# Rounding w_in's blocks on GpSimd, and the first residual and the second solver put earlier

## The chip, the cores and the metric

The kernel runs on one core of a Trainium2 chip. The metric is the device time of one execution in microseconds (us), as the median of several runs. Engines are named as the profile names them: PE (TensorE, matmuls), DVE (VectorE), ACT (ScalarE), POOL (GpSimd) and SP (SyncE, which issues most DMAs). Each engine works through its own instructions in the order in which the program gave them to it.

## What is computed

Three layers follow one another: a delta-rule attention, a gated MLP that mixes over time, and a second MLP with a token shift. Only the start of the program is changed, which is the attention and the first matmul of the second layer:

```python
k_n = k / (np.linalg.norm(k, axis=-1, keepdims=True) + 1e-06)
for t in range(S):                       # B=4, H=8, S=768, D=48
    y[:, :, t] = q_t @ state
    v_old = state.T @ k_t
    state = state + beta_t * outer(k_t, v_t - v_old)
x = y as (B, S, 384)
h = gelu(x @ w_in)                       # w_in is 384 x 1024; u, v = the halves of h
v_n = layernorm(v) * g_ln
x = x + (u * (w_sg @ v_n + b_sg)) @ w_out
...                                      # second MLP with w_k, w_v, w_r
```

## The kernel before, in words

**Attention.** The 768 time steps are cut into 12 chunks of 64 (`s`), the 32 pairs of batch and head into two halves (`o`). Two chunks make a group `g` (six groups). Per group, PE builds Gram matrices of k (`gram`, L331 and L333), ACT copies them to SBUF (L340), and DVE inverts a triangular system per head (`solver`, L358 to L438); its last instruction, a transpose on L438, writes `DT`. `couple(g, k)` (L452, two halves `k`) joins the two 32-wide blocks of a chunk. Then, per chunk and half, five PE stages follow: `st_rq` (products with the state, L493 and L496, and for group 0 the value term, L479), `residual` (a copy by ACT on L468 for group 0, a sum by DVE on L470 later), `st_d` (L516, needs `DT` and the residual `r`), `st_n` (L529, needs the joined block), `st_s` (L544) and `st_y` (L558). ACT copies between them, and POOL masks (L509). `vt[s]` is v times the norm of k, made by POOL in `scale_v` (L460).

**Weights.** The weights come as 64-bit floats. `narrow` makes a high and a low 32-bit part of each block of 128x256: a DMA into `raw` (three buffers), four instructions of DVE on `na` (two buffers; L167, L169, L171, L173), ACT on L162, an exact integer add by POOL (L175), and `split`: the high part by a rounding copy of ACT (L118), the low part by a subtraction of POOL (L121). w_in has twelve such blocks (six `wiv`, then six `wiu`) which stay resident; w_out (eight) and w_k (twelve) follow during the attention, and go back to DRAM.

**Filling.** Between the stages PE does the matmuls of the second layer: `v_units` (L628) and `u_units` (L680), which need the high and low parts `xh` and `xl` of the attention's output (`x_split`) and the w_in blocks. Where there is nothing to fill with, `keep_warm` issues matmuls on zeros (L719).

**What sets the order.** It is written out when the program is built. A counter `point` goes up by one per third of a stage slot; at each point `background` hands DVE's instruction streams (layer norm, solver, weight blocks) an amount of estimated time, shared by the weights of `SHARE`, and runs what is due by `after`. The start (`early`) runs the first solver with the first blocks of w_in; then the slots begin (`tick`, `run`) with the second solver. What the planner estimates doesn't bind the chip: there each engine waits for semaphores alone.

Of the kernel before, what the change touches and what calls it, by code (L numbers as in the profile page):

```python
# [34 lines left out]
SV = 60  # L35
B0 = 1.0
PRE = 0.8
GRAM0 = 17
SOLVE0 = 1
RUN = (3, 2, 3)  # L40
# [8 lines left out]
LAGC = 2  # L49
JS = 18  # L50
NT_ = (3, 3, 3)
LNW = 1
LAGX = 6
LAGE = (4, 1)
LASTP = 134
FROM = 125
LAGU = 5
COST = dict(rq=1.05, d=0.8, n=0.8, s=0.85, y=1.1)
SHARE = ((1, 12, 1), (1, 4, 1), (2, 8, 2))
NRAW = 3  # L60
# [24 lines left out]
def fused_kernel(  # L85
# [66 lines left out]
    def narrow(dram, i, j, hi, lo, cw=CW, pool=stg, lag=JLAG, parts=None):  # L152
# [23 lines left out]
        if hi is None:  # L176
            hi, lo = (raw[:, e * cw:e * cw + cw].bitcast(F32R) for e in range(2))
            parts.append(raw[:, :2 * cw].bitcast(F32).rearrange("p (x n) -> p x n", x=2))
        yield lag, lambda: split(A, G, af, hi, lo)

# [62 lines left out]
    with ExitStack() as at:  # L243
# [112 lines left out]
        def solver(g):  # L356
# [37 lines left out]
            for i in range(1, 8):  # L394
                tv, t = product(32 * i, [(264, 4), (0, i), (1, i)], NT,
                                0, [(64, 4), (8, i), (1, i)], Yt)
                yield t
                yield total(vw(Yt, i, [(64, 4), (8, i)]), tv, t)
            V.tensor_copy(vw(Dm, 0, [(264, 4), (32, 8), (1, 8)]), vw(Yt, 0, [(64, 4), (1, 8), (8, 8)]))
            yield 0.4  # L400
# [18 lines left out]
            for last in (0, 1):  # L419
# [9 lines left out]
                for i, (ov, args) in enumerate(ops):  # L429
                    tv, t = product(*args)  # L430
                    yield t
                    if g == 0 and last and i == 1:
                        V.memset(warm, 0.0)
                    if g == 0 and last and i == 2:
                        scale_v(0)
                    yield total(ov, tv, t)
# [4 lines left out]
            if g:  # L441
                for k in range(2):
                    after(LAGC + k, lambda k=k: couple(g, k))

# [107 lines left out]
        def st_y(s, o):  # L552
# [13 lines left out]
            if s % 2:  # L566
                store_x(g, o, ysts[o])
                after(LAGX if g < NG - 1 else LAGE[o], lambda: splits.append((g, o)))
            if o == 1:
# [25 lines left out]
        def x_split(g, o):  # L595
# [8 lines left out]
            split(A, G if g < NG - 1 else V, xs, xh, xl)  # L604
            after(LAGU, lambda: push(g, o, xh, xl))
            return True
# [85 lines left out]
        def fill(n):  # L692
# [14 lines left out]
            if n > 0 and point[0] < 144:  # L707
                idle[0] += min(n, WARM) if point[0] <= 36 else n
                keep_warm(int(idle[0]))
# [61 lines left out]
        def early(n, t):  # L771
            for _ in range(n):
                background(t)
                while len(running) < 2 and len(jobs) > n_rest:
                    start_job(LJ0 if point[0] else LJ)
# [23 lines left out]
        while any(e[2] == "solve" for e in streams):  # L799
            early(1, PRE)  # L800
            k += 1
            if k == 2:
# [4 lines left out]
                nc.sync.dma_start(out=mu_sb, in_=mu)  # L807
            if 0 in neTs and 1 not in GDs:
                after(SV, lambda: scale_v(1))
                body = st_rq(0, 0)  # L810
                rest.append(lambda: next(body))
                rest += [lambda j=j: whole(j) for j in gram(1)]
            if rest:
                rest.pop(0)()
        for f in rest:
            f()
        next(body, None)
        next(body, None)
        keep_warm(JS)
# [4 lines left out]
        later[:] = [(i, f) for i, (_, f) in enumerate(later)]  # L824
        later += [(3 + k, lambda k=k: couple(0, k)) for k in range(2)]
        used[0] = 0

        def tick():
            g, n = divmod(point[0], 24)
            point[1] = min(g, 1) + 1  # L830
            gg, nn = divmod(point[0] - GRAM0, 24)
            if nn == 0 and 0 <= gg and gg + 2 < NG:
                grams.extend(gram(gg + 2))
            if n == 0 and g + 1 < NG:
                streams.append([point[0] + SOLVE0, solver(g + 1), "solve"])
# [4 lines left out]
            while len(jobs) > n_rest and len(running) < RUN[0]:  # L840
                start_job()
            if grams and (point[0] - GRAM0) % GSTEP == 0:
                for _, f in grams.pop(0):
# [354 lines left out]
```

## Time and profile before

| | us |
|---|---|
| median of 3 runs | 772.91 (771.91 to 774.02) |
| profiled execution, its own time | 771.39 |
| its span, first to last instruction | 769.7 |
| PE busy | 697.1 (91%) |
| DVE busy | 507.0 (66%) |
| ACT busy | 372.9 (48%) |
| POOL busy | 200.6 (26%) |

Busy shares are means over the span. In the stretch from 40 to 120 us DVE is busy for 75.3 of 80 us, and PE for 68.2. A row of a timeline or of the chain of waits gives the start in us, the duration in us, and what ran; "x64" counts instructions, and a bracket gives the engine's idle time before the row and what ended it. In a timeline, the rows of one engine may overlap a little, since an instruction starts before the one ahead has quite ended. In the chain, "issue" is time in which nothing that the profile shows was waited for. A row by stretches gives, after the length, the busy time and the count of PE, of PE's weight loads, of DVE, ACT and POOL, then the granted PE clock as a share of 2.4 GHz, the DMA share and GB/s.

### The profile page before, as it was taken

What the parts mean: (1) busy time and instruction counts of PE and PEld (TensorE: products, weight loads), DVE (VectorE), ACT (ScalarE), POOL (GpSimd) and SP (SyncE); (2) the same over time, 40 slices, a digit from 0 to 9 for tenths busy, and PEclk for the clock granted to TensorE, in tenths of its full rate; (3) what the DMA queues carried; (4) which work ended last, traced back from release to release, by engine and by line L of the source; (5) the groups of instructions that cost most, each with busy time, mean ns of one, the idle gap of its engine ahead of it and who ended that gap; (6) DMA issues with size and microseconds to landing.
All of it is one profiled execution on the core that took longest, in us unless ns stands there. A gap on an engine that the chain in (4) does not pass through costs nothing.

```text
span 769.7 us, 24933 instructions
## 1 busy us (share of the span) xinstructions
PE 697.1 (91%) x10820; PEld 648.8 (84%) x10820; DVE 507.0 (66%) x1071; ACT 372.9 (48%) x752; POOL 200.6 (26%) x246
## 2 busy tenths in 40 slices
PE   3559799898998998888889979999999999999998
PEld 3437688787887886687889979999999999999997
DVE  6989999697797884532286867289564564563441
ACT  3236576766765767653332322147454453462330
POOL 3034635353454554430235341210000000000000
PEclk9978899999999999999989999999999999999999
DMA  8413445565565566556467562327000000000000
GB/s 238 93 41 100 131 123 153 129 185 163 148 185 155 159 171 181 194 149 198 143 229 244 178 195 79 110 87 194 22 11 32 21 11 32 21 10 32 11 22 32
DMA packets 82159, 88.76 MB, mean 115 GB/s; under 512 B 24704, under 2 KB 65024, under 8 KB 82048
## 3 DMA queue, kind: packets, MB, share of 16 engines
q1 hardware_dynamic: 76816, 77.92, 34.2%
q0 software_dynamic: 4800, 9.04, 4.3%
q8 instruction: 85, 1.39, 0.7%
q14 instruction: 26, 0.21, 0.1%
q10 hardware_dynamic: 432, 0.20, 0.1%
HBM read 56.60 MB, written 25.82 MB: 107 GB/s over the span
## 4 chain that ended last, share of the span: by engine, by line
PE 70%; DVE 12%; DMA 5%; issue 4%; POOL 3%; ACT 2%; SPq 1%; POOLq 0%; DVEq 0%; ACTq 0%
PE ms L149 36%; PE ms L944 7%; PE ms L628 6%; PE ms L680 5%; PE ms L558 3%; DVE sg L353 3%; PE rk L516 2%; PE sps L544 2%; PE rk L529 2%; PE rk L493 2%; PE ms L452 2%; POOL na L175 2%; DVE sg L391 1%; PE ms L331 1%; DVE Yt L391 1%
## 5 line engine op out<-in xcount | busy, mean ns | idle before, releaser
L149 PE MATMUL ms<-wvh,sl 128*128 128x384 f32 x192 | 64.6, 336 | 0.0
L149 PE MATMUL ms<-wvl,sh 128*128 128x384 f32 x192 | 64.5, 336 | 0.0
L149 PE MATMUL ms<-wvh,sh 128*128 128x384 f32 x192 | 64.5, 336 | 0.0
L149 PE MATMUL ms<-xm_hi,sw0h 128*128 128x384 f32 x192 | 64.2, 335 | 0.0
L149 PE MATMUL ms<-xm_hi,sw0l 128*128 128x384 f32 x192 | 64.2, 334 | 0.0
L149 PE MATMUL ms<-xm_lo,sw0h 128*128 128x384 f32 x192 | 64.2, 334 | 0.0
L175 POOL TENSOR_TENSOR na<-na,raw 128x256 int32<-128x256 int32 (+2 forms) x43 | 38.4, 894 | 98.3 <-DVE na L173 52.1
L121 DVE TENSOR_TENSOR sl<-sg,sh 128x384 fp32r<-128x384 f32 x64 | 35.7, 557 | 30.3 <-ACT sh L118 30.2
L944 PE MATMUL ms<-sw0h,g 128*128 128x384 f32 x192 | 50.3, 336 | 1.7 <-DVE g L121 1.7
L118 ACT ACTIVATE sh<-sg 128x384 fp32r<-128x384 f32 x64 | 33.5, 524 | 36.3 <-DVE sg L1118 36.3
L944 PE MATMUL ms<-ws1h,g 128*128 128x384 f32 x192 | 49.9, 334 | 0.0
L680 PE MATMUL ms<-xh,wiu_hi 128*128 128x256 f32 x144 | 40.2, 298 | 7.5 <-ACT v L637 7.5
L353 DVE TENSOR_TENSOR sg<-sg,Yt 128x512 f32<-128x512 f32 (+10 forms) x78 | 44.5, 570 | 1.6
L1134 DVE TENSOR_TENSOR sg<-sg,ms 128x384 f32<-128x384 f32 x24 | 13.3, 554 | 46.2 <-PE ms L149 46.2
L1118 DVE TENSOR_TENSOR sg<-sg 128x384 f32<-128x384 f32 x64 | 35.4, 553 | 11.5 <-ACT sg L1117 11.4
L1117 ACT ACTIVATE sg<-ms 128x384 f32<-128x384 f32 x64 | 30.8, 482 | 24.2 <-PE ms L149 24.0
L118 ACT ACTIVATE gh<-w 128x384 fp32r<-128x384 f32 x32 | 16.6, 524 | 53.1 <-DVE w L1031 53.1
L680 PE MATMUL ms<-xh,wiu_lo 128*128 128x256 f32 x144 | 39.6, 294 | 0.0
L680 PE MATMUL ms<-xl,wiu_hi 128*128 128x256 f32 x144 | 39.4, 293 | 0.0
L118 ACT ACTIVATE xm_hi<-sg 128x384 fp32r<-128x384 f32 x48 | 23.4, 517 | 31.7 <-PE ms L149 30.5
L149 PE MATMUL ms<-gh,wo_hi 128*128 128x384 f32 x96 | 34.5, 359 | 4.2 <-ACT gh L118 4.2
L509 POOL TENSOR_SCALAR_AFFINE_SELECT SQ<-SQ 64x512 f32<-64x512 f32 x36 | 27.4, 761 | 38.3 <-ACT SQ L508 32.3
(236 smaller groups left out, 2219.2 us busy)
## 6 DMA issues: line engine op xcount, KB each, us to landing
u_d<-ug SPq DMA_DIRECT2D x24, 256.0 KB, 3.5
u<-u_d SPq DMA_DIRECT2D x16, 384.0 KB, 4.8
vn_d<-v SPq DMA_DIRECT2D x22, 256.0 KB, 3.6
vk<-in_vk_dram SPq DMA_DIRECT2D x24, 192.0 KB, 4.1
vk<-in_vk_dram SPq DMA_DIRECT2D x12, 384.0 KB, 4.8
out_dram<-sg SPq DMA_DIRECT2D x24, 192.0 KB, 1.9
SQ<-in_q_d_dram SPq DMA_DIRECT2D x36, 96.0 KB, 4.3
xT<-yst SPq DMA_DIRECT2D x23, 144.0 KB, 4.1
```

Of the source, the lines that this page charges most:

```text
L118: A.activation(hi, src, AF.Copy)
L121: eng_lo.tensor_tensor(lo, src, hi.bitcast(F32), op=ALU.subtract)
L149: T.matmul(pt, lhsT=a, rhs=b, start=(i == 0), stop=(i == n - 1))
L175: G.tensor_tensor(a.bitcast(I32), a.bitcast(I32), w_lo.bitcast(I32), op=ALU.add)
L353: V.tensor_tensor(tv, vw(a_t, a_off, a_dims), vw(b_t, b_off, b_dims), op=ALU.mult)
L509: G.affine_select(out=pt, in_=pt, pattern=[[0, 8], [1, C]], compare_op=ALU.is_gt, fill=0.0, base=0, channel_multiplier=-1)
L558: T.matmul(yps[b0:b0 + 64, (0, 1, 2, 6, 3, 4, 5, 7)[p], :], lhsT=cur[h][:, p, 0:64], rhs=cur[h][:, p, D:], start=True, stop=True)
L628: T.matmul(vstat[g, b], lhsT=a[:, c], rhs=w[:, c], start=first, stop=last)
L680: T.matmul(vstat["u"][:, 2 * P * d:2 * P * d + 2 * P], lhsT=w[:, c, ds_], rhs=a[:, c].rearrange("p b t -> p (b t)"), start=first, stop=last)
L944: T.matmul(pt[:, :DM], lhsT=v[:, ds_], rhs=w, start=(c == 0 and i == 0), stop=(c == 5 and i == 2))
L1117: A.activation(r, pt[:, :DM], AF.Relu)
L1118: V.tensor_tensor(r, r, r, op=ALU.mult)
```

## The change

It has eight parts.

- In `narrow`, blocks with `lag` 0 (w_in's twelve) get their high part from POOL, by a `tensor_scalar` on L122, where ACT made it before.
- The first `st_rq` is run to its end before the matmuls that keep PE busy, so that ACT's residual copy and its two mask inputs (L469, L509) stand ahead of blocks' work; `scale_v(0)` and the clearing of `warm` come earlier.
- The start takes up three blocks before the first solver, not two.
- The second solver is put at the head of the streams when the slots begin, and weighs 8 instead of 4 against the blocks.
- `couple(0, 1)` comes five points after `couple(0, 0)`; group 1's couples come at points 27 and 32, behind the first stage that needs `DT`.
- The third Gram's four parts come at points 13, 15, 21 and 23 (17, 19, 21 and 23 before).
- `xh` and `xl` of group 0 come earlier.
- Zero matmuls: 44 instead of 18 before the slots, and at most 4 in a slot everywhere.

```diff
-B0 = 1.0
+B0 = 1.05
+GRAMF = (13, 15, 21, 23)
-JS = 18
+JS = 44
+LAG0 = (4, 3)
-SHARE = ((1, 12, 1), (1, 4, 1), (2, 8, 2))
+SHARE = ((1, 12, 1), (1, 8, 1), (2, 8, 2))
...
-        yield lag, lambda: split(A, G, af, hi, lo)
+        yield lag, lambda: split(A if lag else G, G, af, hi, lo)
...
+            if g == 0:
+                V.memset(warm, 0.0)
...
-                    after(LAGC + k, lambda k=k: couple(g, k))
+                    n = LAGC + k if g > 1 else max(LAGC + k, 27 + 5 * k - point[0])
+                    after(n, lambda k=k: couple(g, k))
...
-                idle[0] += min(n, WARM) if point[0] <= 36 else n
+                idle[0] += min(n, WARM)
...
-                while len(running) < 2 and len(jobs) > n_rest:
+                while len(running) < (2 if point[0] else 3) and len(jobs) > n_rest:
...
+                scale_v(0)
                 after(SV, lambda: scale_v(1))
                 body = st_rq(0, 0)
                 rest.append(lambda: next(body))
                 rest += [lambda j=j: whole(j) for j in gram(1)]
+                rest += [lambda: next(body, None)] * 2
...
-        next(body, None)
-        next(body, None)
         keep_warm(JS)
...
-        later += [(3 + k, lambda k=k: couple(0, k)) for k in range(2)]
+        later += [(3 + 5 * k, lambda k=k: couple(0, k)) for k in range(2)]
+        spent[:] = [0] * 3
+        streams.insert(0, [0, solver(1), "solve"])
...
-            if nn == 0 and 0 <= gg and gg + 2 < NG:
+            if point[0] == GRAMF[0]:
+                grams.extend(gram(2))
+            if nn == 0 and 0 < gg and gg + 2 < NG:
```

The first place is ACT's queue around the first residual. `wiv_hi` is a high part, `r` the residual, `rk` and `qk` the PSUM tiles of `st_rq`. Before:

```order
16 L340 ACTIVATE sw0h_112<-ms 128x256
17 L118 ACTIVATE wiv_hi<-na 128x256 x2
18 L468 ACTIVATE r_736<-rk 128x384
19 L508 ACTIVATE sw0h_120<-qk 64x8x64
20 L508 ACTIVATE sw0l_121<-qk 64x8x64
21 L162 ACTIVATE raw<-raw 128x256 x2
22 L521 ACTIVATE u_823<-rk 128x384
```

The same place now:

```order
16 L342 ACTIVATE sw0h_112<-ms 128x256
17 L164 ACTIVATE raw<-raw 128x256
18 L469 ACTIVATE r_704<-rk 128x384
19 L509 ACTIVATE sw0h_120<-qk 64x8x64
20 L509 ACTIVATE sw0l_121<-qk 64x8x64
21 L164 ACTIVATE raw<-raw 128x256 x2
22 L522 ACTIVATE u_866<-rk 128x384
```

The two roundings that stood ahead of the residual's copy have left ACT.

The second place is DVE's queue around the end of the second solver (`STREAM_TRANSPOSE DT`) and the first residual that DVE adds (`r<-vk,rk`), with the start of the third solver behind it (`sg<-sg`). Before:

```order
175 L171 TENSOR_SCALAR na<-na 128x256
176 L438 STREAM_TRANSPOSE DT<-sg_109 128x32x32
177 L167 TENSOR_SCALAR na<-raw 128x256
178 L173 SCALAR_TENSOR_TENSOR na<-raw,na 128x256
179 L470 TENSOR_TENSOR r_1640<-vk,rk 128x384
180 L169 TENSOR_SCALAR na<-na 128x256
181 L171 TENSOR_SCALAR na<-na 128x256
182 L173 SCALAR_TENSOR_TENSOR na<-raw,na 128x256
183 L358 STREAM_TRANSPOSE sg_107<-sg_108 128x1024
```

The same place now, from the row behind `DT`'s transpose (which is row 168):

```order
170 L171 TENSOR_SCALAR na<-na 128x256
171 L173 TENSOR_SCALAR na<-na 128x256
172 L175 SCALAR_TENSOR_TENSOR na<-raw,na 128x256
173 L169 TENSOR_SCALAR na<-raw 128x256
174 L171 TENSOR_SCALAR na<-na 128x256
175 L173 TENSOR_SCALAR na<-na 128x256
176 L175 SCALAR_TENSOR_TENSOR na<-raw,na 128x256
177 L169 TENSOR_SCALAR na<-raw 128x256 x2
178 L171 TENSOR_SCALAR na<-na 128x256 x2
179 L173 TENSOR_SCALAR na<-na 128x256 x2
180 L175 SCALAR_TENSOR_TENSOR na<-raw,na 128x256 x2
181 L471 TENSOR_TENSOR r_1675<-vk,rk 128x384
```

Two instructions of blocks stood between `DT` and the residual before; now sixteen stand there (row 169, the end of a block, is the first), of the last five blocks of w_in.

## Rows read from the trace of the kernel before

**Rows 1.** The chain of waits, from 0 to 345 us.

```profile
92.71 3.63 PE ms L452 x128
...
97.73 1.44 PE rk L516 x64
...
104.05 3.38 PE ms L628 x14
107.42 0.81 PE rk L516 x64
...
241.08 1.13 PE ms L452 x64
...
289.03 2.05 PE ms L719 x9
```

**Rows 2.** Busy time by stretches of the span.

```profile
90.00:92.70 2.70, 0.00 (x0) 0.02 (x1) 2.70 (x5) 1.36 (x3) 1.31 (x2) 0.96 0.53 103
92.70:96.00 3.30, 3.29 (x124) 3.30 (x126) 3.21 (x6) 0.42 (x1) 2.33 (x3) 0.50 0.41 99
107.00:285.00 178.00, 165.03 (x4841) 144.85 (x4839) 148.24 (x332) 119.26 (x234) 84.45 (x102) 0.98 0.58 161
```

**Rows 3.** DVE's timeline, first solver and start of the second.

```profile
14.54 1.25 DVE L358 STREAM_TRANSPOSE sg<-sg 128x1024 f32<-128x1024 f32 x1 [3.51 <-ACT sg L340]
15.82 0.19 DVE L362 TENSOR_SCALAR ss<-sg 128x32 f32<-128x32 f32 x1
...
46.51 1.92 DVE L438 STREAM_TRANSPOSE sw0l<-sg 128x1024 f32<-128x1024 f32 x1
...
52.78 1.23 DVE L358 STREAM_TRANSPOSE sg<-sg 128x1024 f32<-128x1024 f32 x1
```

**Rows 4.** ACT's timeline around the first residual copy.

```profile
49.58 0.42 ACT L118 ACTIVATE wiv_hi<-na 128x256 fp32r<-128x256 f32 x1 [2.92 <-POOL na L175]
49.90 0.47 ACT L468 ACTIVATE r<-rk 128x384 f32<-128x384 f32 x1
```

**Rows 5.** DVE's timeline, second half of the second solver.

```profile
82.46 1.96 DVE L353 TENSOR_TENSOR sg<-sg,Yt 128x512 f32<-128x512 f32 x1
85.05 0.41 DVE L173 SCALAR_TENSOR_TENSOR na<-raw,na 128x256 uint32<-128x256 uint32 x1
85.39 0.95 DVE L353 TENSOR_TENSOR sg<-sg,Yt 128x768 f32<-128x768 f32 x1
...
87.24 0.28 DVE L167 TENSOR_SCALAR na<-raw 128x256 uint32<-128x256 uint32 x1
87.44 1.22 DVE L353 TENSOR_TENSOR sg<-sg,Yt 128x1024 f32<-128x1024 f32 x1
...
90.65 1.92 DVE L438 STREAM_TRANSPOSE DT<-sg 128x1024 f32<-128x1024 f32 x1
...
92.94 0.53 DVE L470 TENSOR_TENSOR r<-vk,rk 128x384 f32<-128x384 f32 x1
```

**Rows 6.** POOL's timeline at the start.

```profile
...
10.84 0.78 POOL L175 TENSOR_TENSOR na<-na,raw 128x256 int32<-128x256 int32 x1 [5.74 <-DVE na L173]
12.15 0.73 POOL L121 TENSOR_TENSOR wiv_lo<-na,wiv_hi 128x256 fp32r<-128x256 f32 x1 [0.53 <-ACT wiv_hi L118]
...
14.76 0.31 POOL L359 MEMSET Yt<- 128x256 f32 x1
```

**Rows 7.** POOL's timeline in the second solver.

```profile
82.34 1.53 POOL L460 TENSOR_TENSOR vk<-vk,neT 128x768 f32<-128x768 f32 x1
85.55 1.39 POOL L175 TENSOR_TENSOR na<-na,raw 128x256 int32<-128x256 int32 x1 [1.68 <-DVE na L173]
```

**Rows 8.** ACT's timeline at the end of the attention.

```profile
332.19 0.42 ACT L118 ACTIVATE raw<-na 128x256 fp32r<-128x256 f32 x1 [1.37 <-POOL na L175]
332.63 0.60 ACT L637 ACTIVATE v<-ms 128x512 f32<-128x512 f32 x1
```

**Rows 9.** PE's waits from 326 to 340 us: total, times, longest.

```profile
PE ms L558 <- ACT v L637: 1.1, 1, 1.1
```

More of the change, by code (lines that the diff above doesn't have):

```diff
@@ L431, in solver @@
                     yield t
[L432 to L435, printed above, removed]
                     yield total(ov, tv, t)
@@ L567, in st_y @@
                 store_x(g, o, ysts[o])
-                after(LAGX if g < NG - 1 else LAGE[o], lambda: splits.append((g, o)))
+                after((LAGX if g else LAG0[0]) if g < NG - 1 else LAGE[o],
+                      lambda: splits.append((g, o)))
             if o == 1:
@@ L604, in x_split @@
             split(A, G if g < NG - 1 else V, xs, xh, xl)
-            after(LAGU, lambda: push(g, o, xh, xl))
+            after(LAGU if g else LAG0[1], lambda: push(g, o, xh, xl))
             return True
@@ L831, in tick @@
             gg, nn = divmod(point[0] - GRAM0, 24)
-            if nn == 0 and 0 <= gg and gg + 2 < NG:
+            if point[0] == GRAMF[0]:
+                grams.extend(gram(2))
+            if nn == 0 and 0 < gg and gg + 2 < NG:
                 grams.extend(gram(gg + 2))
-            if n == 0 and g + 1 < NG:
+            if n == 0 and 0 < g < NG - 1:
                 streams.append([point[0] + SOLVE0, solver(g + 1), "solve"])
@@ L841, in tick @@
                 start_job()
-            if grams and (point[0] - GRAM0) % GSTEP == 0:
+            if grams and (point[0] in GRAMF if g == 0 else (point[0] - GRAM0) % GSTEP == 0):
                 for _, f in grams.pop(0):
```

## The prediction

> **What bounds the kernel now.** I read the chain of waits first, since it names the engine that is late at each time. Up to 92.7 us it runs over DVE: the first solver takes from 14.54 to 48.43 (its last row starts at 46.51 and lasts 1.92), the second from 52.78 to 92.57 [rows 3, 5]. Then it passes to PE: the couples start at 92.71, 0.14 behind `DT`, and the first stage that needs that `DT` at 97.73 [rows 1]. Busy time by stretches tells what follows: from 107 to 285 us PE is busy for 165 of 178 us [rows 2], with DVE at 148 and ACT at 119 beside it, so PE is the bound there, and what is won ahead of 107 us should come out at the end, one for one. From about 290 us on, ACT, POOL and DMAs are waited for in places; the change reaches one of these, PE's wait of 1.1 us for ACT's copy on L637 [rows 9].
>
> One more thing is to be seen in the stretches: PE's clock. From 90 to 92.7 us PE does nothing; in the 3.3 us behind that idle time the granted clock is 0.50 (1.2 GHz), against 0.98 from 107 us on [rows 2]. The 128 couple matmuls take 3.63 us there; 64 of them take 1.13 at full clock, and the 64 of L516 take 1.44 at 97.73 against 0.81 at 107.42 [rows 1]. So an idle PE ahead of the first `DT` is paid for again behind it.
>
> So three things decide: when the second solver ends, how long the first residual behind it takes, and what PE does meanwhile.
>
> **The rounding on POOL.** Before, POOL never makes the high part. Its nearest rows at this size are a clearing of 128x256 in 0.31 and an add with two inputs in 0.78, elsewhere 0.73 for the subtraction [rows 6]. An operation with one input lies between these. I take 0.44, nearer to the clearing, since both touch fewer tiles than the add, with 0.31 and 0.73 as the ends; it is an estimate. It saves a trip to ACT: the subtraction waited 0.53 for ACT [rows 6], which goes. A block on POOL is then 0.73 + 0.44 + 0.73 and small gaps, 2.0 us (1.8 to 2.3). A gain for ACT itself I price at nothing here: ACT is not what is waited for before 107 us, other than at the next point.
>
> **The first residual copy.** PE's first L516 came behind ACT's copy at 49.90, which ends at 50.37; that copy stood behind two roundings, the last of which waited 2.92 for POOL [rows 4]. The order shows these roundings gone, so now `DT` of the first solver is what is late. It comes later than 48.43, because a third block's four instructions stand ahead of the solver and two of its blocks' steps need POOL to have let go of `na`: POOL starts on the first block at 10.84 [rows 6], so block one takes until about 12.9, where L358 started at 14.54 and the next one followed at 15.82 [rows 3]. I take 1.5 us for the start and 0.5 for later blocks and masks that are in the way: first `DT` at 50.4 (48.4 if all is covered, 51.5 if POOL blocks DVE more). That is as late as the copy was: no gain, no loss for PE's first L516.
>
> **The second solver.** Before it ran 39.8 us (52.78 to 92.57). At its head in the streams and with the weight 8, it has nine instructions of blocks fewer inside: five of `tensor_scalar` at 0.20 (87.24 to 87.44) and four of L173 at 0.34 (85.05 to 85.39) [rows 5], 2.3 us. Then there are products that took longer beside POOL: L353 with 512 columns took 1.96 at 82.46, where 768 took 0.95 and 1024 took 1.22 [rows 5], while POOL's multiplication on L460 ran for 1.53 from 82.34 [rows 7]. The other way, POOL's add of 0.73 took 1.39 at 85.55, over L353's 0.95 from 85.39 [rows 5, 7]. With fewer blocks of POOL inside, and `scale_v(1)` still there, I count 1.0 us of it as gone. So 39.8 - 2.3 - 1.0 = 36.5. In the order it follows the first `DT` with a small instruction or two between, so it starts some 0.45 behind it, at 50.85, where it was 4.35 before. Second `DT` at 87.3 (85 to 88.5), against 92.57: 5.2 us earlier.
>
> The Trainium skill, "SBUF — State Buffer", section "Who interferes with whom", calls the port pair that DVE and GpSimd share an exclusive lock: an operation of one that holds it blocks the other's for its whole length. The 1.96 and the 1.39 agree with this. By that rule a rounding on POOL blocks DVE where ACT's didn't, which speaks against the change: at 0.44 for each of the two or three roundings in a solver the sum would be about 1 us later for each solver, inside the bounds above.
>
> **The blocks behind the solver.** Here the order shows what the first look misses. Between `DT` and L470 stood two instructions, and the residual followed at 92.94, 0.4 behind `DT`. Now sixteen stand there, eleven `tensor_scalar` and five L175, of the last five blocks. DVE's own time for them is only 11 x 0.20 + 5 x 0.34 = 3.9 us. But `na` has two buffers, and a buffer is free only when POOL has done with the block in it. So POOL's 2.0 us per block set the speed: 0.4 for the first block's last step, three blocks of POOL, 6.0, the last pair's DVE work of about 1.75 once the buffer is free, and the residual's own 0.53 [rows 5], with some 0.5 of blocking: 9.2 (8.3 to 10.2). The residual is there at 87.3 + 9.2 = 96.5, and L516 with it, against 97.73: of 5.2 us that the solver wins, 1.2 stay. PE had nothing left at 90 us before [rows 2], and in the order it has less ahead of that L516 now (no couples, four zero matmuls per slot at most). So I expect it to idle for some 10 us, and to run at the low clock behind that.
>
> **From that L516 to the next half's.** Before, 9.69 us (97.73 to 107.42) [rows 1]. The couples now stand behind the first L516: 2 x 1.13 = 2.26 more at full clock. Four zero matmuls fewer are 0.91 less (2.05 / 9 each [rows 1]), one L628 more, 0.24 (3.38 / 14 [rows 1]). 11.28, and about 1.0 for the low clock: the pair of couples took 3.63 against 2.26 and L516 1.44 against 0.81 [rows 1], 2.0 in all, of which the stretch before had its half already. So the second half's L516 comes at 96.5 + 11.3 + 1.0 = 108.8 against 107.42: 1.4 us later. With the ends of each term the shift at this point lies between -2.8 and +4.6 (both are worked out under the rivals). The third Gram's earlier parts, and `xh` and `xl` of group 0, move work within this stretch that nobody had waited for: I take nothing, and 0.5 each way. If L628 came to wait for POOL's `xl`, its wait would be part of POOL's time in the second rival.
>
> **The end of the attention.** At 332.19 the last rounding of w_k stood ahead of ACT's L637, and had waited 1.37 for POOL [rows 8]; PE waited 1.1 for that copy [rows 9]. In the new order that rounding stands some copies earlier in ACT's queue, and L637's copy has no block's step just ahead of it. That wait goes: -1.1. The zero matmuls there (2.05 for nine at 289.03 [rows 1]) are limited to four per slot now: seven fewer in this part, 7 x 0.228 = 1.6, of which more than half had lain in PE's idle time: -0.7. Together -1.8 (-0.9 to -2.4).
>
> **The sum.** The profiled execution took 771.39, 1.52 below the median of 772.91. 771.39 + 1.4 - 1.8 = 771.0; against the median 772.5.
>
> **The rivals.** *The block burst is short.* POOL's rounding near 0.31, no blocking, a second `DT` at 85, the residual 8.3 behind it, at 93.3, and no more time at the low clock than before: L516 of the second half comes at 93.3 + 11.3 = 104.6, a shift of -2.8, the end gives -1.8 to -2.4, and the time is near 768.0 against the median. For it: nine instructions gone from the solver are sure, and 4 us less between the two solvers too. Against it: PE has no more work ahead of L516 in either case, so it idles for 8 us.
>
> *POOL becomes the bound*, and the kernel is slower. This is the burst behind the second solver: POOL's rounding costs 0.73 like its other instructions, and DVE's instructions meet POOL's; a block is then 2.3, second `DT` at 88.5, the residual 10.2 behind it, and L516 at 98.7, behind an idle time that keeps PE at 1.2 GHz for couples and stages (2.0): 98.7 + 11.3 + 2.0 = 112.0 at the second half, +4.6, less 1.4 at the end: +3.2, near 776. It decides from a residual at about 98 us: 98 + 13.3 is +3.9, less 1.4 is the 2.3 or so that can be told from nothing. For it: the 1.39 and 1.96 where both meet [rows 5, 7]; against it: without waits for ACT each block of POOL's is 0.53 shorter.
>
> By the rule of the Trainium skill's page named above each of the five roundings in the burst would block a DVE instruction, 5 x 0.44 to 5 x 0.73, and the forecast would be 774.7 to 776.2.
>
> *The early part is hidden*: the residual's gain and its cost cancel, and what is seen is the late -1.8 alone, 771.1 against the median. It counts with "no difference" below.
>
> **How the numbers follow.** This measurement tells about 0.3%, 2.3 us, from no change, so faster is below 770.6 and slower above 775.2. My forecast and the hidden case hold 0.41 together, and mean 771 to 775. The short burst has 0.33: some of its parts are sure, and the forecast is itself below the median. POOL as the bound has 0.26. Bounds of the sum: shift -2.8 with -2.4 at the end gives 767.7; shift +4.6 with -0.9 gives 776.6. These hold 8 in 10, since what is left out is that several ends meet on one side.
>
> **What would show it.** In the profile of the changed kernel: twelve roundings of POOL on L122, near 0.44; L438 ending near 50.4 and 87.3; L471 near 96 with waits of DVE for POOL in the ten us ahead of it; PE idle about 10 us ahead of L516's successor, and its granted clock low behind that; no wait for ACT on L637's successor near 330 us. Wrong would be: sixteen instructions that pass in under 6 us (then it is faster), roundings above 1 us on POOL (slower), or a residual behind 99 us.

## The result and the profile of the changed kernel

The changed kernel is slower: 777.72 us (median of 20 runs) against 773.56 for the kernel before in the same comparison, a ratio of 1.0052 with a 95% interval of 1.0028 to 1.0075, or about 4 us. I had forecast 772.5, no difference that can be told, in a range of 767.7 to 776.6. The profiled execution took 779.96, 2.2 above its median, where that of the kernel before was 2.2 below; so the two traces lie 8.6 us apart, and a single position in them is worth no more than some microseconds. The ratios in this text leave out runs more than 1.5% above the fastest of their kernel, eight of the 35 of the kernel before that were taken beside e1 to e4 and two of e10's twelve; by the medians of all runs e2 is at 1.0060 and e10 at 0.9965.

| us, from the two traces | before | forecast | changed |
|---|---|---|---|
| end of the first `DT` | 48.43 | 50.4 | 51.36 |
| end of the second `DT` | 92.57 | 87.3 | 87.35 |
| first residual that DVE adds, end | 93.47 | 96.5 | 97.77 |
| L516/L517 of that half | 97.73 | 96.5 | 97.83 |
| the same stage of the other half | 107.42 | 108.8 | 116.2 |
| end of the third `DT` | 136.50 | none | 146.14 |
| the ninth of these stages, first to need the third `DT` | 145.3 | none | 153.4 |

So the second solver ended where I had worked it out, to 0.05 us. All that it won was gone at the first stage behind it, and at the same stage of the other half the changed kernel is 8.8 us late. DVE's timeline of the changed kernel shows the first part of the loss (start, duration, instruction, in the bracket what it waited for); the rows answer to [rows 5].

```profile
85.39 1.96 DVE L438 STREAM_TRANSPOSE DT<-sg 128x1024 f32<-128x1024 f32 x1
87.20 0.41 DVE L175 SCALAR_TENSOR_TENSOR na<-raw,na 128x256 uint32<-128x256 uint32 x1
...
90.20 0.81 DVE L169 TENSOR_SCALAR na<-raw 128x256 uint32<-128x256 uint32 x1 [1.02 <-POOL wiu_lo L123]
...
91.98 0.92 DVE L175 SCALAR_TENSOR_TENSOR na<-raw,na 128x256 uint32<-128x256 uint32 x1
92.82 0.28 DVE L169 TENSOR_SCALAR na<-raw 128x256 uint32<-128x256 uint32 x1
95.54 0.29 DVE L169 TENSOR_SCALAR na<-raw 128x256 uint32<-128x256 uint32 x1 [2.44 <-POOL wiu_lo L123]
...
97.22 0.55 DVE L471 TENSOR_TENSOR r<-vk,rk 128x384 f32<-128x384 f32 x1
97.69 1.24 DVE L360 STREAM_TRANSPOSE sg<-sg 128x1024 f32<-128x1024 f32 x1
```

DVE has the sixteen block instructions between `DT` and the residual, and stands still twice, 1.02 and 2.44 us, until POOL lets go of a `na` buffer. The third solver (L360) stands behind the same rows: it starts at 97.69, where it started at 94.74 before. POOL's timeline of the same stretch, which answers to [rows 7]:

```profile
90.13 0.74 POOL L177 TENSOR_TENSOR na<-na,raw 128x256 int32<-128x256 int32 x1
90.95 0.85 POOL L122 TENSOR_SCALAR wiu_hi<-na 128x256 fp32r<-128x256 f32 x1
91.89 0.73 POOL L123 TENSOR_TENSOR wiu_lo<-na,wiu_hi 128x256 fp32r<-128x256 f32 x1
93.03 0.73 POOL L177 TENSOR_TENSOR na<-na,raw 128x256 int32<-128x256 int32 x1 [0.41 <-issue]
...
102.78 0.66 POOL L510 TENSOR_SCALAR_AFFINE_SELECT sw0l<-sw0l 64x512 f32<-64x512 f32 x1
103.52 1.73 POOL L123 TENSOR_TENSOR xl<-xT,xh 128x768 fp32r<-128x768 f32 x1
```

A rounding takes 0.85, a block 2.5 us or more (90.13 to 93.03 with a gap). POOL works through five blocks and two masks, with two waits of 0.41 and 1.60 us between, and `xl`, which the filling matmuls of PE need, comes last, at 105.25. ACT stands still too, since its own block step waits for a load:

```profile
92.06 0.44 ACT L164 ACTIVATE raw<-raw 128x256 int32<-128x256 uint32 x1 [3.68 <-DMA raw<-in_w_in_dram]
94.23 0.44 ACT L164 ACTIVATE raw<-raw 128x256 int32<-128x256 uint32 x1 [1.73 <-DMA raw<-in_w_in_dram]
```

What PE waited for from 85 to 120 us (total, times, longest):

```profile
PE rk L517 <- DVE r L471: 5.2, 1, 5.2
...
PE ms L630 <- POOL xl L123: 0.9, 1, 0.9
```

And the stretches of the same time (length; busy time and count of PE, PE's weight loads, DVE, ACT, POOL; then the granted clock as a share of 2.4 GHz):

```profile
92.00:98.00 6.00, 0.78 (x13) 0.27 (x15) 3.56 (x11) 4.09 (x9) 3.73 (x6) 0.79 0.50 138
98.00:102.00 4.00, 4.00 (x120) 3.79 (x118) 3.83 (x10) 2.21 (x5) 3.75 (x5) 0.50 0.32 84
102.00:104.00 2.00, 2.00 (x80) 1.82 (x76) 1.90 (x6) 0.84 (x2) 1.85 (x4) 0.92 0.48 147
104.00:106.00 2.00, 1.07 (x5) 0.56 (x4) 1.93 (x5) 0.93 (x2) 1.50 (x2) 0.93 0.37 80
106.00:116.00 10.00, 10.00 (x172) 7.99 (x170) 9.03 (x30) 6.42 (x11) 4.68 (x6) 0.50 0.59 156
116.00:120.00 4.00, 4.00 (x135) 3.52 (x135) 3.97 (x7) 2.31 (x6) 1.49 (x1) 1.00 0.16 53
```

PE is idle for 5.2 us, runs at 1.2 GHz (0.50) to 102, gets the full clock back, waits 0.93 us for `xl`, and runs at 1.2 GHz again for all of 106 to 116, though it is busy without a gap there. In the kernel before, the clock is 1.00 from 100 to 120 us, and PE is busy for all of that time.

### The profile page after: what moved, and what is told of

Read it like the earlier page. It is cut to its first block, busy times and chain, and to the rows that moved or that the text cites. A ratio compares the mean times of both kernels' runs of the same rounds, so it can differ in the third digit from the quotient of the medians.

```text
span 778.2 us, 24964 instructions
## 1 busy us (share of the span) xinstructions
PE 707.7 (91%) x10836; PEld 655.8 (84%) x10836; DVE 508.2 (65%) x1071; ACT 368.8 (47%) x740; POOL 212.2 (27%) x258
## 2 busy tenths in 40 slices
DMA packets 82158, 88.76 MB, mean 114 GB/s; under 512 B 24704, under 2 KB 65024, under 8 KB 82048
## 4 chain that ended last, share of the span: by engine, by line
PE 68%; DVE 5%; DMA 5%; issue 3%; POOL 3%; ACT 2%; SPq 1%; POOLq 0%; DVEq 0%
PE ms L151 35%; PE ms L950 7%; PE ms L682 6%; PE ms L630 6%; PE ms L559 3%; PE rk L530 2%; PE rk L517 2%; PE rk L494 2%; PE sps L545 2%; PE ms L453 1%; DMA raw<-in_w_r_dram 1%; PE ms L333 1%; POOL na L177 1%; DMA raw<-in_w_v_dram 1%; DVE gl L123 1%
## 5 line engine op out<-in xcount | busy, mean ns | idle before, releaser
L1124 DVE TENSOR_TENSOR sg<-sg 128x384 f32<-128x384 f32 x64 | 35.4, 553 | 11.5 <-ACT sg L1123 11.4
L355 DVE TENSOR_TENSOR sg<-sg,Yt 128x512 f32<-128x512 f32 (+10 forms) x78 | 41.5, 532 | 1.8
L164 ACT ACTIVATE raw<-raw 128x256 int32<-128x256 uint32 (+2 forms) x43 | 19.5, 453 | 41.5 <-DMA raw<-in_w_v_dram 19.4
L169 DVE TENSOR_SCALAR na<-raw 128x256 uint32<-128x256 uint32 (+2 forms) x43 | 19.9, 463 | 29.1 <-DMA raw<-in_w_v_dram 16.4
## 6 DMA issues: line engine op xcount, KB each, us to landing
xT<-yst SPq DMA_DIRECT2D x23, 144.0 KB, 3.6
```

The source lines that it names most:

```text
L355: V.tensor_tensor(tv, vw(a_t, a_off, a_dims), vw(b_t, b_off, b_dims), op=ALU.mult)
L1124: V.tensor_tensor(r, r, r, op=ALU.mult)
```

## The experiments

Four theories stand in the expectations below. A: the late residual is the loss, since POOL's blocks hold up DVE. B: PE's clock behind the idle time is. C: the couples that were moved behind the first stage are. D, formed after the first four runs: what counts is DVE, which runs three solvers one behind the other up to the third `DT`; blocks that stop DVE there are the loss. (The traces don't bear out the last step of D, as the next section shows: PE waits for the third `DT` in none of them.) All ratios are to the kernel before, measured beside it on the same chip, with their 95% intervals. Three chips were used, one for e1 to e4, one for e5 to e8 and one for e9 to e12, so runs of different groups are compared by way of the kernel before. To compare the runs, the positions of their traces stand in one table:

| kernel | second `DT` | first stage | other half | third `DT` | ninth stage | ratio |
|---|---|---|---|---|---|---|
| before | 92.57 | 97.7 | 107.4 | 136.5 | 145.3 | 1 |
| changed | 87.35 | 97.8 | 116.2 | 146.1 | 153.4 | 1.0052 (1.0028 to 1.0075) |
| e1_act_round | 86.65 | 98.0 | 110.9 | 144.0 | 152.5 | 1.0064 (1.0035 to 1.0093) |
| e2_sums | 87.89 | 97.5 | 117.7 | 145.1 | 155.0 | 1.0103 (1.0064 to 1.0141) |
| e3_warm | 88.76 | 99.2 | 118.0 | 147.9 | 157.4 | 1.0017 (0.9990 to 1.0044) |
| e4_couple | 89.01 | 103.0 | 114.8 | 147.2 | 154.1 | 1.0043 (1.0012 to 1.0075) |
| e5_nosolve | 97.96 | 98.7 | 111.9 | 143.0 | 149.4 | 1.0009 (0.9978 to 1.0040) |
| e6_nna3 | 87.22 | 97.1 | 115.5 | 145.5 | 156.5 | 1.0040 (1.0004 to 1.0075) |
| e7_b_solver | 86.10 | 97.1 | 116.1 | 148.3 | 157.6 | 1.0131 (1.0091 to 1.0172) |
| e8_b_poolround | 95.50 | 100.6 | 111.1 | 140.1 | 152.1 | 1.0064 (1.0038 to 1.0090) |
| e9_others | 96.31 | 97.1 | 110.5 | 143.7 | 151.9 | 1.0013 (0.9978 to 1.0049) |
| e10_sh3_act | 95.79 | 96.2 | 108.5 | 139.5 | 147.0 | 0.9955 (0.9920 to 0.9990) |
| e11_sh3_pool | 97.29 | 97.7 | 109.2 | 141.7 | 149.5 | 0.9995 (0.9961 to 1.0029) |
| e12_b_sh3 | 97.68 | 99.9 | 111.9 | 141.6 | 151.2 | 1.0036 (1.0007 to 1.0066) |

**The roundings by ACT again (e1).**

```diff
-        yield lag, lambda: split(A if lag else G, G, af, hi, lo)
+        yield lag, lambda: split(A, G, af, hi, lo)
```

> The changed kernel with the high parts of w_in rounded by ACT again, as before; all else as changed. Theory A (the late residual: POOL's instructions, with a rounding that takes 0.85 us and not 0.44, hold up the sixteen block instructions of DVE, so the residual is ready at 97.8): a block costs POOL 0.73 + 0.53 of waiting for ACT + 0.73 = 2.0 instead of 2.5, so the first solver ends some 0.5 us earlier, the residual some 1.5 to 2 us earlier (near 96), and the whole kernel is 1.5 to 2.5 us faster than the changed one. Theory B (the clock: PE's idle time ahead of that stage puts it at 1.2 GHz for most of 98 to 116 us, which costs some 6 us): PE's idle time is a little shorter but stays over 3 us, so the clock is as low as before and nothing more than those 2 us is won.

Not faster: 1.0064. The first solver ended 0.8 us earlier, where 0.5 was expected, but the residual hardly (97.52), since it waited for PE's L497 now, and the third solver for ACT's Gram copies:

```profile
93.42 0.29 DVE L169 TENSOR_SCALAR na<-raw 128x256 uint32<-128x256 uint32 x1 [1.89 <-POOL wiu_lo L123]
...
96.96 0.56 DVE L471 TENSOR_TENSOR r<-vk,rk 128x384 f32<-128x384 f32 x1 [1.77 <-PE qk L497]
...
98.71 1.25 DVE L360 STREAM_TRANSPOSE sg<-sg 128x1024 f32<-128x1024 f32 x1 [1.20 <-ACT sg L342]
```

PE's clock was 1.00 from 98 to 120 us, and the other half's stage came 5.3 us earlier than in the changed kernel. Yet the whole was no faster. By the ninth stage 0.9 us of the 5.3 were left, and at the twentieth of these stages this trace was 4.1 us behind the changed kernel's (291.07 against 286.93). From the other half's stage to that one it took 9.5 us longer; for 7.2 of these PE was idle, mostly in waits of the kind "issue". So neither taking POOL's roundings back nor the 5 us won at 116 showed at the end, and why the 5 us were lost again is open.

**The residual out of DVE's queue (e2).**

```diff
-SUMS = (0,)
+SUMS = (0, 1)
```

> The changed kernel with the residuals of group 1 made as those of group 0: PE adds the value term (one more matmul of 0.9 us in each of four stages, 3.6 us of PE) and ACT copies, so that no residual of group 1 stands in DVE's queue behind the sixteen block instructions. Theory A (late residual) and B (clock): the first stage that needs the second DT starts near 93.5 us instead of 97.8, PE is idle for under 1 us ahead of it, its clock stays at 2.4 GHz, and the same stage of the other half comes near 106 instead of 116: 10 us earlier there, less 2 to 3 us of matmuls later, so 5 to 8 us faster than the changed kernel. If the order of PE's work (couples behind that stage, theory C) and not the wait is the loss, the other half's stage comes near 112 and the kernel is about as slow as the changed one.

This fell: the first stage started at 97.5, and the kernel was 1% slower than the one before (the added matmuls, L480, keep PE busy for 4.4 us of that). ACT's timeline says why:

```profile
92.33 0.46 ACT L164 ACTIVATE raw<-raw 128x256 int32<-128x256 uint32 x1 [3.83 <-POOL wiu_hi L122]
94.78 0.43 ACT L164 ACTIVATE raw<-raw 128x256 int32<-128x256 uint32 x1 [2.00 <-DMA raw<-in_w_in_dram]
...
96.93 0.49 ACT L469 ACTIVATE r<-rk 128x384 f32<-128x384 f32 x1
```

The same blocks stand in ACT's queue, which waits 3.83 and 2.00 us for their buffers and loads. Going round DVE doesn't help: the burst stops three engines. (Three buffers `raw` are loaded again only when POOL has added a block.)

**Zero matmuls in the idle time (e3).**

```diff
         def st_d(s, o):
+            if (s, o) == (2, 0):
+                keep_warm(20)
```

> The changed kernel with 20 more zero matmuls on PE just ahead of the first stage that needs the second DT (20 x 0.228 = 4.6 us, in an idle time of 5.2 us). Theory B (clock): that stage still starts near 97.8, but the clock there is 1.0, and it and the next stages are done 3 to 4 us earlier (the other half's stage near 112 to 113 instead of 116; if the later wait of 0.9 us for POOL then doesn't lower the clock again, near 110); the kernel is 3 to 6 us faster than the changed one. Theory A alone (only the wait itself counts): no earlier, within 1 us of the changed kernel.

PE's clock was 1.00 from 92 to 104 us, as meant, and the other half's stage came at 118.0, no earlier than in the changed kernel. PE's waits from 85 to 120 us show where the gain went:

```profile
PE ms L632 <- POOL xl L123: 2.9, 1, 2.9
PE rk L519 <- DVE r L471: 2.3, 1, 2.3
```

The wait for `xl` grew from 0.9 to 2.9, and the clock fell behind it as before:

```profile
104.00:106.00 2.00, 0.00 (x0) 0.00 (x0) 1.93 (x5) 0.42 (x1) 1.85 (x3) 0.93 0.61 159
106.00:116.00 10.00, 9.29 (x169) 7.76 (x170) 8.62 (x32) 4.68 (x9) 4.57 (x7) 0.50 0.63 160
```

So theory B has the right sign for the low clock, but what is late there is POOL. The ratio of 1.0017 can't be told from the changed kernel's nor from 1.

**The couples back (e4).**

```diff
-                    n = LAGC + k if g > 1 else max(LAGC + k, 27 + 5 * k - point[0])
+                    n = LAGC + k
```

> The changed kernel with group 1's couples put back to two points behind the second solver, ahead of the first stage that needs DT. Theory C (the couples' move puts 2 x 1.2 us of PE work out of an idle time and onto the path): the first stage still starts near 97.8, the other half's stage comes 2.5 to 3.5 us earlier (near 113), and the kernel is about 3 us faster than the changed one. Theory B (clock): PE works from 87 to some 95 us, idles 3 us less, and the clock may stay up too: then 4 to 7 us. Theory A alone: no gain.

No difference from the changed kernel that can be told (1.0043). The couples now stood ahead of the third Gram's matmuls, PE waited 7.1 us for `DT` with these behind it, and the first stage came at 103.0, the other half's at 114.8. Theory C is not borne out.

**The second solver's place undone (e5), and that place alone (e7).**

```diff
-SHARE = ((1, 12, 1), (1, 8, 1), (2, 8, 2))
+SHARE = ((1, 12, 1), (1, 4, 1), (2, 8, 2))
...
-        streams.insert(0, [0, solver(1), "solve"])
...
-            if n == 0 and 0 < g < NG - 1:
+            if n == 0 and g + 1 < NG:
```

> The changed kernel with the second solver's place undone (it joins the streams one slot later, behind the blocks, and weighs 4 as before): all else as changed, POOL's roundings included. Theory D (the blocks that the second solver pushed ahead of the residual and of the third solver make DVE wait some 3.5 us for POOL's release of na, start the third solver 3 us later, and let PE wait for its DT at 146 instead of 136 us): the blocks go back into the second solver, DT of it comes later (near 93), the third solver starts near 95 and ends near 138, the ninth stage that needs a DT (145.3 before, 153.4 changed) comes at 146 to 148, and the kernel is some 4 us faster than the changed one, within 2 us of the kernel before. If POOL's rounding, the couples or the zero matmuls are the loss, the kernel stays 4 us slower than before.

The ratio is 1.0009, which can't be told from the kernel before; its interval overlaps the changed kernel's too. The second `DT` is 10.6 us later than in the changed kernel, and the third 3.2 us earlier. (The third came at 143.0, not at 138.) The counterpart puts the same three lines of the change, and the reset of `spent`, into the kernel before:

```diff
-SHARE = ((1, 12, 1), (1, 4, 1), (2, 8, 2))
+SHARE = ((1, 12, 1), (1, 8, 1), (2, 8, 2))
...
+        spent[:] = [0] * 3
+        streams.insert(0, [0, solver(1), "solve"])
...
-            if n == 0 and g + 1 < NG:
+            if n == 0 and 0 < g < NG - 1:
```

> The kernel before with one part of the change alone: the second solver at the head of the streams when the slots begin, weight 8. Roundings by ACT, couples, zero matmuls and Grams as before. Theory D: second DT near 87, then the same burst of blocks, third solver near 98, and the kernel is 3 to 6 us slower than before. If the early second DT is worth what it seems and the loss came from another part, it is as fast as before or up to 3 us faster.

1.0131: this part alone costs 10 us, though it brings the second `DT` at 86.10. DVE's waits between 88 and 102 us in that run:

```profile
88.45 0.81 DVE L167 TENSOR_SCALAR na<-raw 128x256 uint32<-128x256 uint32 x1 [0.68 <-POOL wiu_lo L121]
...
94.14 0.29 DVE L167 TENSOR_SCALAR na<-raw 128x256 uint32<-128x256 uint32 x1 [3.36 <-DMA raw<-in_w_in_dram]
...
94.82 0.29 DVE L167 TENSOR_SCALAR na<-raw 128x256 uint32<-128x256 uint32 x1 [0.39 <-DMA raw<-in_w_in_dram]
...
96.28 0.56 DVE L470 TENSOR_TENSOR r<-vk,rk 128x384 f32<-128x384 f32 x1 [0.35 <-PE qk L496]
...
101.18 0.81 DVE L167 TENSOR_SCALAR na<-raw 128x256 uint32<-128x256 uint32 x1 [3.68 <-POOL wiu_lo L121]
```

8.5 us of DVE's time go in waits for block buffers and a residual's input, and the third solver starts at 102.56. The residual of the other half stands behind that start in DVE's queue, and here PE does wait for DVE:

```profile
PE rk L516 <- DVE r L470: 5.7, 1, 5.7
```

**Three `na` buffers (e6).**

```diff
-NNA = 2
+NNA = 3
```

> The changed kernel with three na buffers instead of two; the order of every engine is the same. Theory D: DVE's waits of 1.0 and 2.4 us for POOL in the block burst shrink (the raw buffers' loads and POOL's own 2.5 us per block stay), the residual comes 2 to 3 us earlier (95) and the third solver with it; the kernel is 1.5 to 3 us faster than the changed one. If POOL is the bound there itself (five blocks of 2.5 us, then masks and xl), PE's wait for xl at 105 us stays and the gain is under 1 us.

The residual came 0.7 us earlier, not 2 to 3, and the ratio (1.0040) can't be told from the changed kernel's. The wait for `na` became one for `raw`:

```profile
94.29 0.80 DVE L169 TENSOR_SCALAR na<-raw 128x256 uint32<-128x256 uint32 x1 [2.45 <-DMA raw<-in_w_in_dram]
...
96.49 0.54 DVE L471 TENSOR_TENSOR r<-vk,rk 128x384 f32<-128x384 f32 x1
```

**POOL's roundings alone (e8).**

```diff
-        yield lag, lambda: split(A, G, af, hi, lo)
+        yield lag, lambda: split(A if lag else G, G, af, hi, lo)
```

> The kernel before with one part of the change alone: the high parts of w_in's twelve blocks rounded by POOL (0.85 us each without a neighbour, ACT's took 0.42 and a wait of 0.53 for the subtraction): 0.35 us more of POOL per block, 4 us over twelve blocks, of which only what stands ahead of DVE or PE counts. Theory D: within 1.5 us of the kernel before, the first DT 0.5 to 1 us later, the first residual's copy by ACT earlier than before. If POOL's rounding is itself the loss: 3 to 5 us slower.

1.0064, so the roundings alone cost 5 us, which theory D had not foreseen. The second solver started 1.7 us later (54.47 against 52.78) and took 41.0 us instead of 39.8; the second `DT` came 2.9 us later, and PE's first stage behind it too (100.6 against 97.7). That explains a part only.

**What is left without both (e9).** The changes of e1 and e5 together, on the changed kernel.

> The changed kernel with two parts undone: the second solver's place and weight (as in the run that undid it alone) and POOL's roundings (ACT makes them again). What is left of the change: three blocks at the start, the early first residual, the couples, the third Gram, the split of group 0 and the zero matmuls. Theory D (only what holds up DVE counts: it runs three solvers one behind the other until about 137 us, and both the block burst and POOL's roundings make it wait): second DT at 94 to 96 instead of 98, third DT near 138 to 140 instead of 143, and the kernel is 2 to 4 us faster than with the solver's place undone alone, so 0 to 4 us faster than the kernel before. If POOL's roundings cost nothing here (rival), it is the same as that run, within 2 us of the kernel before.

1.0013, the same as e5: beside the rest of the change ACT's roundings gain nothing that can be told, though they cost 5 us in the kernel before. Why is open.

**The head place with a smaller weight (e10, e11, e12).** With the weight 3 instead of 8 the blocks stay inside the second solver: 28 block instructions of DVE by the trace of e10, where the kernel before has 21 and the changed one 12. e11 changes this number alone in the changed kernel, e10 has ACT's roundings too, and e12 is e7 with that weight.

```diff
-SHARE = ((1, 12, 1), (1, 8, 1), (2, 8, 2))
+SHARE = ((1, 12, 1), (1, 3, 1), (2, 8, 2))
```

> The changed kernel with ACT's roundings and with the second solver at the head of the streams but with the weight 3 instead of 8: 29 block instructions inside the second solver (28 before, 13 changed), none between its DT and the residual (2 before, 16 changed). Theory D: the solver starts near 51, second DT near 91 to 92, the residual right behind it, third solver near 93 and its DT near 136; the kernel is 1 to 5 us faster than the kernel before, and 6 to 9 us faster than the changed kernel with ACT's roundings. If the head place itself is the loss and not the burst: no faster than that kernel.

0.9955: 0.45% faster than the kernel before (0.1 to 0.8%), and against e1, which differs in the weight alone, 1.1%, with intervals that don't meet. DVE's rows at the end of the second solver show no wait:

```profile
93.84 1.95 DVE L438 STREAM_TRANSPOSE DT<-sg 128x1024 f32<-128x1024 f32 x1
95.63 0.54 DVE L471 TENSOR_TENSOR r<-vk,rk 128x384 f32<-128x384 f32 x1
96.08 1.24 DVE L360 STREAM_TRANSPOSE sg<-sg 128x1024 f32<-128x1024 f32 x1
```

The second `DT` is 8.4 us later than in the changed kernel, and the third 6.6 us earlier; both came some 4 us later than expected. PE's idle time ahead of the first stage is 1.5 us, its clock is 1.00 from 84 to 160 us:

```profile
92.00:98.00 6.00, 4.53 (x199) 3.54 (x195) 5.90 (x9) 4.21 (x9) 2.78 (x4) 1.00 0.45 103
```

Where e10's gain over the kernel before arises its trace doesn't show: it reaches the twentieth stage 0.8 us earlier than the trace of the kernel before and the first matmuls of the next part 1.8 us later (341.06 against 339.29), and what follows there, which the change doesn't touch, took the least time of all these traces.

> The changed kernel with one number changed: the weight of the second solver 3 instead of 8, POOL's roundings kept. Theory D: as the run with ACT's roundings, but DVE waits for POOL in the second solver: its DT near 94 to 95 instead of 91 to 92, the kernel 2 to 4 us slower than that run and 2 to 5 us faster than the changed kernel. Rival (roundings cost nothing here): the same as that run.

0.9995: one number of the changed kernel takes back its loss (the intervals of the two, 0.9961 to 1.0029 and 1.0028 to 1.0075, just touch). The second `DT` came at 97.3, later than the 94 to 95 expected. POOL's roundings cost some 3 us against e10 by the ratios (2.2 by the medians), with intervals that overlap.

> The kernel before with the second solver at the head of the streams with the weight 3 (31 block instructions inside it, none between its DT and the residual), nothing else changed. Theory D: what made the same place with the weight 8 cost 1.3% is the burst of blocks alone, so here the loss is gone: third DT near 136 to 139, within 0.3% of the kernel before or up to 0.4% faster. If the head place itself is the loss and the other parts of the change made up for it in the run with ACT's roundings: 0.5 to 1% slower than before.

1.0036, so this fell in part: against e7 almost 1% is won, but the head place is not free in the kernel before. The second `DT` came at 97.7, later than in e10 (95.8): inside the second solver DVE waited 5.5 us for POOL to let go of `na`, and 0.7 in e10. The third came at 141.6, not at 136 to 139. So e10's gain needs other parts of the change too; which of them was not tried, nor was `B0` (a little more of DVE's work per point at the start, in the diff but not among the eight parts), which e7 and e12 lack. e10 is the only version whose interval lies below the kernel before, and its upper end is 0.999.

## Why the prediction was wrong

**What bounds the kernel.** I took PE as the bound from 107 to 285 us [rows 2], and let a shift at 107 us pass to the end. The two traces bear this out: every wait of PE in that stretch, before and changed, is of the kind "issue", and none is for another engine. DVE, busy for 148 of the 178 us, comes near. I never looked at its third solver, whose `DT` is 9.6 us late in the changed kernel. The transpose that ends it, in DVE's timeline, and the couples that need it, in the chain of waits; first the kernel before:

```profile
134.49 2.01 DVE L438 STREAM_TRANSPOSE sw0l<-sg 128x1024 f32<-128x1024 f32 x1
...
139.39 0.04 PE rk L493 x2
139.45 1.38 PE ms L452 x78
```

And the changed kernel:

```profile
144.14 2.00 DVE L438 STREAM_TRANSPOSE sw0l<-sg 128x1024 f32<-128x1024 f32 x1
...
147.85 0.04 PE rk L494 x2
147.91 1.07 PE ms L453 x60
```

PE comes to these couples straight from other matmuls, 2.9 us behind the third `DT` before and 1.7 us behind it now. In the traces of all fourteen kernels it is 1.4 to 5.8 us, and PE is busy right up to it. So the third `DT` held up no PE, and its lateness is not what made the kernel slower: it started 2.95 us later and took 48.45 us instead of 41.76, with sixteen block instructions inside instead of eleven and with 3.3 us of waiting for PE ahead of its residuals. PE's own delay passes on as I had assumed. It is 8.8 us at the other half's stage, 8.1 at the ninth, 7.3 at the twentieth and 5.1 at the first matmuls of the next part.

That the second solver's place and weight are the loss is shown by the pairs e5 and changed, e10 and e1, and e7 and e12. In each the second `DT` is 9 to 12 us later, the other half's stage 2 to 4 us earlier, the third `DT` 3 to 7 us earlier, and the kernel faster by 0.4 to 1.1%; in the first pair the intervals overlap. Neither position gives the time over all runs: e8 and e12 have the third `DT` at 140.1 and 141.6 and are slower than e5 with 143.0, and e3, with the latest stage of the other half, is at 1.0017.

**The second solver.** 36.5 us worked out, 35.75 measured (51.60 to 87.35). The mechanism was right: nine block instructions fewer inside. That its end came out to 0.05 us is luck, since it started 0.75 us later than worked out and took 0.75 us less. That it is a loss to finish it early, since the blocks must follow at once, was in the text as the burst; the residual behind the burst was priced nearly right, and what PE pays behind that was not.

**The rounding on POOL** was mis-sized: 0.44 with ends of 0.31 and 0.73, measured 0.85 where nothing ran beside it, and 0.90 and 1.00 on the mean:

```profile
L122 POOL TENSOR_SCALAR wiu_hi<-na 128x256 fp32r<-128x256 f32 x6 | 6.0, 997 | 0.5
L122 POOL TENSOR_SCALAR wiv_hi<-na 128x256 fp32r<-128x256 f32 x6 | 5.4, 900 | 0.5
```

My upper bound, the nearest instruction with two inputs, was no bound. A block took 2.5 us of POOL, not 2.0, and the residual came 10.4 us behind `DT`, not 9.2 (8.3 to 10.2).

**From that stage to the other half's.** This is the step that failed. I had 12.3 us, 11.3 of matmuls and 1.0 for the low clock (0 to 2.0), and it was 18.3. The stretch in the changed kernel, and below it the same stretch in e10, with the same matmuls at full clock:

```profile
97.83:116.16 18.33, 17.40 (x367) 14.33 (x367) 17.02 (x48) 10.74 (x19) 12.02 (x16) 0.60 0.49 128
96.23:108.53 12.30, 11.30 (x368) 9.43 (x368) 11.44 (x43) 7.76 (x16) 5.23 (x7) 1.00 0.53 135
```

The sum of the matmuls was right, 11.3. The low clock cost 6.1 us (17.40 against 11.30) and not 1.0, and the wait for POOL's `xl`, which I had put at nothing and set aside as part of the second rival, is the other 0.9. I had thought of one idle time with a low clock behind it; there were two, of 5.2 and 0.9 us, and the clock was low from 98 to 102 and again from 106 to 116 us. With the residual 1.3 us later than worked out, this makes the shift at the other half's stage 8.8 us and not 1.4, and the stretch behind it took back 3.7 of these up to 345 us, not 1.8. How much of the 4 us at the end is owed to the low clock alone stays open: e3 kept the first fall of the clock away and only moved the wait to `xl`, and e1 had no fall there and was no faster.

The second rival, POOL as the bound, is nearest to what happened, with the place, the sign and its condition right (a residual at about 98 us; it ended at 97.77), and the price (3.2 us, 776) near the measured 4. That is in part luck: its shift at the other half's stage was 4.6, and the measured one 8.8.

While POOL made `xl` from 103.52 to 105.25, DVE's L140 with two inputs took 1.56 at 103.73, where its neighbours of the same shape took 0.19:

```profile
103.51 0.19 DVE L138 TENSOR_TENSOR rn_t<-rn_y 128x32 f32<-128x32 f32 x1
103.73 1.56 DVE L140 TENSOR_TENSOR rn_t<-rn_t,rn_h 128x32 f32<-128x32 f32 x1
105.33 0.19 DVE L142 SCALAR_TENSOR_TENSOR rn_y<-rn_t,rn_y 128x32 f32<-128x32 f32 x1
```

This is what the Trainium skill states ("SBUF — State Buffer", section "Who interferes with whom": the shared ports are an exclusive lock), and the trace agrees. By that rule I had worked out 774.7 to 776.2, above my forecast and still below the 777.7 measured.

**The first part and the end.** The first `DT` came at 51.36 (50.4 worked out, 48.4 to 51.5 given), and the stage behind it 1.1 us later than before: right in kind. At the end the stretch from the twentieth of these stages (279.60 and 286.93) to the first matmuls of the next part (339.29 and 344.35) is 2.3 us shorter, for 1.8 worked out; PE's wait for ACT's copy ahead of L558 is gone, as I had said. By 345 us the changed trace is 5.1 us behind, which is near the 4 us of the medians. The other 3.5 us of the two traces' distance arise behind that, in code that the change doesn't touch. In the traces of all these kernels the time of the execution less the start of the last of the stages lies between 435.9 (e10) and 442.8 us, so I make nothing of it.

## What to carry to other kernels

Where two streams of work share an engine, what the one gains by going first the other takes back right behind it: ask what is queued after the burst, on each engine that it passes. Price every idle time of the engine that is the bound, the short ones too, together with the clock behind it: here the low clock behind two of them, of 5.2 and 0.9 us, cost 6.1 us. A result that comes late is no loss yet: before it is called one, read whether the engine that needs it waited. The third `DT` came 9.6 us later here, and PE never waited for it. Work with few buffers was cheap here as long as it was spread among other work, and it set the pace of three engines when it was put in one place.

## What the runs showed of the hardware

A rounding copy of POOL with one input took longer (0.85) than its add or subtraction with two (0.73) of the same size; the rows above show both.

PE's clock can fall behind a short wait: after 0.93 us ahead of the `xl` matmuls of the changed kernel it was 1.2 GHz from 106 to 116 us, with PE busy all of that time. The idle time ahead of the first stage had been 5.2 us, and there the clock was low from 98 to 102. In e10 PE was idle for 1.5 us ahead of the same stage, and its clock stayed at 1.00. What makes the difference the traces don't show.

All traces have waits of PE that nothing in the profile explains ("issue"): between 107 and 331 us they sum up to 13.4 us in the kernel before, 11.4 in the changed one and 17.7 in e1. So positions in two traces can differ by some microseconds for this reason alone.
